# Conversion steps moved by one slot, and the first head pair's q and k turned in another order

## The chip, the cores and the metric

The kernel runs on one core of a Trainium2 chip. The metric is the device time in microseconds (us) of one execution. Below, PE is TensorE (matrix products), DVE is VectorE, ACT is ScalarE, POOL is GpSimd, and SP is SyncE, which only issues DMAs here.

## The reference

Attention with a threshold in place of a plain softmax, and then a two-layer MLP with an exact GELU on all tokens:

```python
batch, n_heads, seq, head_dim = (8, 8, 576, 64)
scores = np.matmul(q, k.transpose(0, 1, 3, 2)) / np.sqrt(64)
thresh = np.max(scores, axis=-1, keepdims=True) - tau
scores = np.where(scores >= thresh, scores, -1e9)
attn = np.exp(scores - max)                 # max: of each row
attn = attn / (np.sum(attn, axis=-1, keepdims=True) + 1e-09)
attn_out = np.matmul(attn, v)
x = attn_out.transpose(0, 2, 1, 3).reshape(8 * 576, 512)
h = x @ w_in                                # 512 x 2048
out = (0.5 * h * (1.0 + erf(h / sqrt(2)))) @ w_out   # 2048 x 512
```

The inputs q, k, v and tau are float32; the weights `moe_w_in` and `moe_w_out` are float64, and the kernel gets them as 64-bit words.

## The kernel before, in words

**Pairs and slots.** Two heads are worked on together: a head pair has 2 x 64 = 128 partitions, and there are 32 pairs, four for each batch. A row block of 128 queries is a chunk; the 576 queries of a head make four chunks and a tail of 64, and the tails of both heads share one chunk (chunk 4). A slot is one chunk of one pair. The program is written out slot by slot in a loop over `n`. The first four pairs (batch 0, "early") are done in two passes: slots 0 to 7 take chunks 0 and 1 of pairs 0 to 3, slots 8 to 19 chunks 2, 3 and 4 of pairs 0 to 3. From slot 20 on, each pair has five slots of its own.

**Work of a slot.** `scores` (line L432) multiplies the chunk's q with all k into PSUM, one bank pair for each head; there are two such buffers, so the scores of a slot wait until the slot before has read its own. `softmax_head` then takes the negative row maximum on DVE (L444, `nmx`), the threshold on POOL (L447, `thr`) and the exponential on ACT (L449). `softmax_tail` masks and sums on DVE (L465), which is the last reader of the scores. The result `p` is turned by PE products (L373) and copied by ACT (L380 to L395) into `pT`, and `weigh_v` multiplies it with v (L603, or L635 for half a block). Between these, `fill` puts in products of the MLP's first layer (L703, `hT`) and second layer (L718, `o_ps`), as many as a plan of due work (`GOAL`) allows. The first layer's results of the first block are kept until slot 20, where ACT loads another function table and does eight GELUs (L676), which the first L718 need.

**Turning q and k of the early pairs.** q and k arrive with tokens in partitions and must have the head dimension there. `turn_qk_early` does it with products by the identity (L324) into a PSUM bank `tr`, 8 calls (16 products in the profile) for each of q and k. The result is copied out: q by ACT with a scale (L327, `qT`), k by DVE for pair zero and by ACT else (L329, `kT`). The 64 tail rows are turned into another bank (L336 for zeros, L341), and ACT copies them out: twice for k (L344, L345), once for q (L348, `q_tail`). For pair zero, k comes first, then the tails, then q in two halves with a copy each; for the other pairs, q, k and the tails come in this order. The scale `q_scale` is worked out on DVE from `tau` (L1118 to L1122), which arrives by a DMA that POOL issues. Eight memsets on DVE (L1129) clear the q tails and the last column of v.

**Conversion of the weights.** A weight of 64 bits is turned into float32 on the chip, in 32 pieces of 128 x 512 numbers: 16 of w_in, 16 of w_out. One conversion step is L200 and L201 on ACT (`convert_first`), L208 and L209 on DVE (`convert_second`), and an addition L220 on POOL (`add_low_bits`). ACT's part runs one piece ahead. After DVE's part the next piece is loaded (`load_piece`, L184, issued by SP); eight loads are issued before the first conversion. POOL's additions belong to the next slot: the newest one right after its first row maximum and ahead of its threshold, the rest after the exponentials. How many steps stand at the end of slot `n` is written in a list:

```python
STEPS = [0, 1, 1, 1, 1, 1, 1, 1, 1, 2, 2, 2, 3, 2, 2, 3, 3, 3, 1, 0, 1]
```

In slots 12, 15 and 18, `convert_ahead(STEPS[n] - 1)` puts ACT's part earlier in the slot when more than one step is due.

**Order.** Nothing is scheduled by a tool: each engine runs its instructions in the order of the program, and waits by semaphores. In slots 18 and 19, DVE also turns k and q of pair 4 (L410; L415 and L420), which the scores of slot 20 need.

After slot 159 the last ten blocks of 256 tokens go through the MLP by nested Strassen-like products (L891), with sums on DVE and POOL (L773). The change doesn't reach that part.

Of the kernel before, what the change touches and what calls it, by code (L numbers as in the profile page):

```python
# [8 lines left out]
FP32 = mybir.dt.float32  # L9
U32 = mybir.dt.uint32  # L10
U8 = mybir.dt.uint8
AF = mybir.ActivationFunctionType
# [6 lines left out]
def kernel(  # L19
# [40 lines left out]
    TAIL = S - MAIN  # L60
# [19 lines left out]
    ps = ctx.enter_context(tc.tile_pool(name="ps", bufs=4, space=PSUM))  # L80
# [33 lines left out]
    def x_rows(i):  # L114
        return xall[:, i, :, :].rearrange("p c t -> p (c t)")
# [5 lines left out]
    ident = const.tile([P, P], FP32, name="ident")  # L121
# [3 lines left out]
    q_tail = [att.tile([P, P], FP32, name=f"q_tail{i}") for i in range(4)]  # L125
    v_sb = [att.tile([P, 2, KR, D], FP32, name=f"v{i}") for i in range(4)]
# [11 lines left out]
    q_scale = const.tile([P, 1], FP32, name="q_scale")  # L138
# [126 lines left out]
    def load_early(p):  # L265
        b, hp = divmod(p, HP)
        s = st[p] = {}
        for name, src in (("q", q), ("k", k)):

            if p == 2:  # L270
                at = s[name + "_slot"] = x_slot()
                t = x_rows(at)[:, 0:2 * (NC + 1) * D].rearrange("p (e c d) -> p e c d", e=2, d=D)
            else:
                t = ld.tile([P, 2, NC + 1, D], FP32, tag=name, name=name)
            s[name] = t
            eng = (nc.scalar, nc.gpsimd)[p] if p < 2 and name == "k" else nc.sync
# [23 lines left out]
    def turn_qk_early(p, names="qk"):  # L300


        s = st[p]
        if names == "k":
            qT, kT = s["qT"], s["kT"]
        elif 2 <= p < HP:
            qT = op.tile([P, MAIN], FP32, tag="o_sb", name="qT")
            kT = pd_tail[p - 2].rearrange("p b i -> p (b i)")
        else:
            qT = ld.tile([P, MAIN], FP32, tag="qT", name="qT")  # L310
            kT = ld.tile([P, TAIL + S], FP32, tag="kT", name="kT")
        s["qT"], s["kT"] = qT, kT
        qt = s["q_tail"] = q_tail[p % 4]
        copy = nc.scalar.copy if p else nc.vector.tensor_copy
        tiles = {name: s.pop(name) for name in names}

        def most(name, parts=1):
            t = tiles[name]
            tr = ps.tile([P, NC, P], FP32, tag="mm", name="tr")
            n = NC // parts  # L320
            for part in range(parts):
                for c in range(part * n, (part + 1) * n):
                    for e in range(2):
                        nc.tensor.matmul(tr[e * D:(e + 1) * D, c, :], lhsT=t[:, e, c, :], rhs=ident, start=True, stop=True)  # L324
                src = tr[:, part * n:(part + 1) * n, :].rearrange("p c s -> p (c s)")
                if name == "q":
                    nc.scalar.activation(qT[:, part * n * P:(part + 1) * n * P], src, AF.Copy, bias=0.0, scale=q_scale)  # L327
                else:
                    copy(kT[:, TAIL:S], src)  # L329

        def tails():
            tr = ps.tile([P, NC, P], FP32, tag="mm", name="tr")
            if "q" in names:
                none = q_tail[HP - 1][0:TAIL, D:2 * D]
                for e in range(2):
                    nc.tensor.matmul(tr[e * D:(e + 1) * D, 0, (1 - e) * TAIL:(2 - e) * TAIL], lhsT=ident[0:TAIL, 0:D],  # L336
                                     rhs=none, start=True, stop=True)
            for j, name in enumerate(names):
                for e in range(2):
                    at = e * TAIL if name == "q" else 0  # L340
                    nc.tensor.matmul(tr[e * D:(e + 1) * D, j, at:at + TAIL], lhsT=tiles[name][0:TAIL, e, NC, :],  # L341
                                     rhs=ident[0:TAIL, 0:TAIL], start=True, stop=True)
            if "k" in names:
                nc.scalar.copy(kT[:, S:S + TAIL], tr[:, j, 0:TAIL])  # L344
                nc.scalar.copy(kT[D:P, 0:TAIL], tr[D:P, j, 0:TAIL])  # L345
            if "q" in names:
                yield
                nc.scalar.activation(qt, tr[:, 0, :], AF.Copy, bias=0.0, scale=q_scale)  # L348
# [12 lines left out]
        x_free.extend(s.pop(name + "_slot") for name in names if name + "_slot" in s)  # L361

    def turn_p_early(p, i, later=None):

# [760 lines left out]
    load_early(2)  # L1125
    for _ in range(4):
        load_piece(nc.sync)
    for t in q_tail + [t[:, :, NC, :] for t in v_sb]:
        nc.vector.memset(t, 0.0)  # L1129
    turn_qk_early(0)  # L1130
    load_v_early(0)
    load_early(3)
# [2 lines left out]
    parts = [(range(2), HP), (range(2, SLOTS), HP)] + [(range(SLOTS), 1)] * (NP - HP)  # L1135
# [33 lines left out]
    for n in range(len(slots) + WEIGH + 1):  # L1169
        p, i = slots[n] if n < len(slots) else divmod(n, SLOTS)  # L1170
# [33 lines left out]
        if long:  # L1204
            convert_ahead(STEPS[n] - 1)
        if n in DIVIDE_LATE:
# [120 lines left out]
```

## Time and profile before

| | |
|---|---|
| runs shown, us | 1331.37, 1327.67, 1330.39; median 1330.39 |
| profiled execution, us | 1327.03 |
| its span, first to last instruction, us | 1325.3 |
| granted clock of PE | 1.000 |

The profile is of one execution, with times from the start of its span. Busy time is the time in which an engine executes an instruction; PE's busy time is modelled, since its products are pipelined. In a line of the timeline the columns are the start, the time from the first instruction's start to the last one's end, the engine, the line of the kernel's file, the operation, what it writes and reads, the shape, the number of instructions, and in brackets the idle time of the engine just ahead with what ended it, where there was any. The window 0 to 8.71 us, until the first scores, has PE busy for 6.83 us; from 98.76 to 105.57 us, between the scores of slots 17 and 18, it is busy for 5.00 of 6.81 us.

### The profile page before, as it was taken

The page shows a single profiled execution, that of the slowest core. Times are in us where ns is not written, and L with a number is a line of the kernel's source. Part 1 is how long each engine was busy: PE and PEld are TensorE (multiplying, and loading weights), DVE is VectorE, ACT ScalarE, POOL GpSimd, SP SyncE. Part 2 cuts the span into 40 slices and gives each one's busy share as a digit, 9 for nine tenths or more (in the row PEclk, how much of TensorE's full clock was granted, in tenths as well). Part 3 has the DMA queues.
Part 4 walks back from the last instruction along what each step waited for, and adds up shares of the span by engine and source line. Part 5 has one row for each costly group of instructions (what it writes and reads, how often), then busy time and mean ns, then how long its engine had stood idle before and what let it go on. Part 6 is the DMA issues. An engine that isn't in the chain of part 4 may idle for free.

```text
span 1325.3 us, 19980 instructions
## 1 busy us (share of the span) xinstructions
PE 1313.4 (99%) x6362; PEld 890.3 (67%) x6362; DVE 1042.8 (79%) x2009; ACT 601.9 (45%) x1018; POOL 634.2 (48%) x1058
## 2 busy tenths in 40 slices
PE   9999999999999999999999999999999999999998
PEld 7775476576476466466466466478778787877877
DVE  6888877888888888888888888883857698386674
ACT  7888266376376367357457438232111203211120
POOL 3565555465555555565555541236364403645430
PEclk9999999999999999999999999999999999999999
DMA  8453676767777777787787775400000140000003
GB/s 256 161 178 106 145 164 159 166 156 168 189 164 164 191 181 165 193 190 168 184 192 170 176 165 115 100 9 0 1 1 0 40 110 11 0 1 0 1 0 80
DMA packets 213688, 153.14 MB, mean 116 GB/s; under 512 B 117264, under 2 KB 196992, under 8 KB 213584
## 3 DMA queue, kind: packets, MB, share of 16 engines
q1 hardware_dynamic: 195440, 125.31, 40.4%
q0 software_dynamic: 17712, 26.26, 7.5%
q8 instruction: 52, 0.85, 0.3%
q14 instruction: 52, 0.43, 0.1%
q10 hardware_dynamic: 432, 0.30, 0.1%
HBM read 56.62 MB, written 12.58 MB: 52 GB/s over the span
## 4 chain that ended last, share of the span: by engine, by line
PE 93%; DVE 2%; issue 1%; DMA 1%; ACT 1%; POOL 1%; SPq 0%; POOLq 0%; DVEq 0%; ACTq 0%
PE bank L891 34%; PE o_ps L718 17%; PE hT L703 16%; PE sc L432 13%; PE xT L603 11%; PE tr L373 1%; DVE nmx L444 1%; PE xT L635 1%; PE tr L324 1%; DVE power L209 1%; DVE power L208 0%; ACT p L449 0%; DVE p L465 0%; DMA inv<-turned 0%; DMA turned_p<-in_moe_w_out_dram 0%
## 5 line engine op out<-in xcount | busy, mean ns | idle before, releaser
L449 ACT ACTIVATE p<-sc,nmx 128x576 f32<-128x576 f32 x288 | 201.9, 737 | 280.0 <-DVE nmx L444 279.8
L465 DVE SCALAR_TENSOR_TENSOR p<-sc,thr,p 128x576 f32<-128x576 f32 x288 | 225.2, 815 | 70.6 <-ACT p L449 62.2
L447 POOL TENSOR_SCALAR thr<-nmx,tau_eff 128x1 f32<-128x1 f32 x288 | 83.9, 293 | 333.3 <-DVE nmx L444 331.2
L703 PE MATMUL hT<-xall,w_in 128*128 128x256 f32 x1024 | 241.8, 385 | 0.0
L444 DVE TENSOR_REDUCE nmx<-sc 128x1 f32<-128x576 f32 x288 | 205.4, 750 | 41.9 <-PE sc L432 40.7
L718 PE MATMUL o_ps<-w_out,g 128*128 128x512 f32 x512 | 236.8, 603 | 0.0
L703 PEld LDWEIGHTS hT<-xall,w_in 128*128 128x128 f32 x1024 | 189.4, 190 | 51.3 <-issue 24.0
L773 DVE TENSOR_TENSOR o<-o,bank 128x256 f32<-128x256 f32 (+1 forms) x242 | 100.1, 417 | 94.5 <-PE bank L891 89.5
L773 DVE TENSOR_TENSOR c<-c,bank 128x320 f32<-128x320 f32 x304 | 147.2, 487 | 33.7 <-PE bank L891 20.1
L718 PEld LDWEIGHTS o_ps<-w_out,g 128*128 128x128 f32 x512 | 93.1, 190 | 109.5 <-issue 107.2
L432 PE MATMUL sc<-kT,qT 64*128 64x288 f32 x960 | 160.1, 429 | 1.5 <-DVE p L465 1.4
L564 DVE STREAM_TRANSPOSE turned_p<-p 128x1152 f32<-128x1152 f32 x112 | 154.4, 1378 | 3.9
L603 PE MATMUL xT<-pT,v 128*64 128x320 f32 (+1 forms) x1200 | 153.6, 410 | 0.0
L432 PEld LDWEIGHTS sc<-kT,qT 64*128 64x128 f32 x960 | 91.2, 186 | 75.9 <-issue 61.1
L603 PEld LDWEIGHTS xT<-pT,v 128*64 128x64 f32 x1200 | 83.4, 137 | 68.0 <-issue 10.4
L891 PE MATMUL bank<-w_out,c 128*128 128x256 f32 (+1 forms) x484 | 120.5, 379 | 0.8 <-DVE o L773 0.8
L261 POOL DMA_DIRECT2D v<-in_v_dram x208 | 110.8, 536 | 3.6 <-issue 1.4
L891 PEld LDWEIGHTS bank<-w_out,c 128*128 128x128 f32 x484 | 90.3, 190 | 19.0 <-DVE o L773 3.2
L958 ACT ACTIVATE c<-c 128x320 f32<-128x320 f32 (+1 forms) x80 | 46.8, 623 | 114.7 <-DVE c L773 114.7
L773 POOL TENSOR_TENSOR c<-c,g 128x320 f32<-128x320 f32 (+1 forms) x40 | 50.5, 1271 | 67.5 <-DVE c L773 67.5
L891 PE MATMUL bank<-t_out,g 128*128 128x256 f32 (+1 forms) x324 | 82.4, 377 | 0.4 <-DVE o L773 0.4
L891 PE MATMUL bank<-t_out,c 128*128 128x256 f32 x320 | 82.7, 381 | 0.0
(188 smaller groups left out, 1755.9 us busy)
## 6 DMA issues: line engine op xcount, KB each, us to landing
pT<-turned_p SPq DMA_DIRECT2D x448, 160.0 KB, 3.5
pT<-pd_tail SPq DMA_DIRECT2D x112, 80.0 KB, 3.0
q<-in_q_dram POOLq DMA_DIRECT2D x104, 72.0 KB, 3.7
k<-in_k_dram POOLq DMA_DIRECT2D x104, 72.0 KB, 3.2
inv<-turned SPq DMA_DIRECT2D x54, 128.0 KB, 4.1
v<-in_v_dram POOLq DMA_DIRECT2D x156, 40.0 KB, 3.1
out_dram<-o SPq DMA_DIRECT2D x40, 128.0 KB, 2.4
xall<-in_moe_w_out_dram SPq DMA_DIRECT2D x9, 512.0 KB, 4.8
```

Source lines behind the costliest of these rows:

```text
L261: eng.dma_start(t[r:P:4, e, 0:n, :], rows[:, r * KR:r * KR + n, :])
L432: nc.tensor.matmul(sc[e][:, h, 0:HALF], lhsT=lhsT, rhs=s["kT"][rows, at:at + HALF], start=True, stop=True)
L444: nc.vector.tensor_reduce(nmx[:, e:e + 1], sc, axis=AXIS.XY, op=ALU.max, negate=True)
L447: nc.gpsimd.tensor_scalar(thr[:, e:e + 1], nmx[:, e:e + 1], -1.0, tau_eff, op0=ALU.mult, op1=ALU.subtract)
L449: nc.scalar.activation(w[:, e * S:(e + 1) * S].rearrange("p (h s) -> p h s", h=2), sc, AF.Exp, bias=nmx[:, e:e + 1], scale=1.0)
L465: nc.vector.scalar_tensor_tensor(row, sc[e][:, :, 0:HALF], thr[:, e:e + 1], row, op0=ALU.is_ge, op1=ALU.mult, accum_out=den[e])
L564: nc.vector.transpose(turned_p[:, :, i // 2, 0:NB, i % 2 * Q:(i % 2 + 1) * Q], w.rearrange("p (e b i) -> p e b i", e=2, i=Q))
L603: nc.tensor.matmul(to, lhsT=s["v"][:, e, c, :], rhs=rhs, start=(c == 0), stop=(c == KR - 1))
L703: nc.tensor.matmul(hT[:, j % 2, :], lhsT=w_in_sb[c][:, j * P:(j + 1) * P], rhs=x_blk[n][:, c, :], start=(c == 0), stop=(c == N_DM - 1))
L718: nc.tensor.matmul(o[:, 0:d_model], lhsT=g[j][:, m * P:(m + 1) * P], rhs=w_out_sb[j], start=(j == 0), stop=(j == N_DF - 1))
L773: eng.tensor_tensor(out, a, b, op=ALU.add)
L891: nc.tensor.matmul(to, lhsT=l, rhs=r, start=start and k == 0, stop=k == len(pairs) - 1, skip_group_check=not start)
```

## The change

Three edits. In the list of conversion steps, slots 16 and 17 have two steps instead of three, slot 18 two instead of one, and slot 19 one instead of none. Pair zero is turned like the other pairs: q first with one copy, then k, then the tails; k's copy stays on DVE. The eight memsets on DVE move ahead of the four instructions that work out `q_scale` and `tau_eff`.

```diff
         copy = nc.scalar.copy if p else nc.vector.tensor_copy
-        tiles = {name: s.pop(name) for name in names}
-
-        def most(name, parts=1):
-            t = tiles[name]
+        for name in names:
+            t = s[name]
             tr = ps.tile([P, NC, P], FP32, tag="mm", name="tr")
...
-        if p == 0:
-            most("k")
-            rest = tails()
-            next(rest)
-            most("q", 2)
-            next(rest, None)
-            return
-        for name in names:
-            most(name)
-        for _ in tails():
-            pass
...
     load_early(0)
+    for t in q_tail + [t[:, :, NC, :] for t in v_sb]:
+        nc.vector.memset(t, 0.0)
     some = const.tile([P, 1], FP32, name="some")
...
-    for t in q_tail + [t[:, :, NC, :] for t in v_sb]:
-        nc.vector.memset(t, 0.0)
     turn_qk_early(0)
...
-    STEPS = [0, 1, 1, 1, 1, 1, 1, 1, 1, 2, 2, 2, 3, 2, 2, 3, 3, 3, 1, 0, 1]
+    STEPS = [0, 1, 1, 1, 1, 1, 1, 1, 1, 2, 2, 2, 3, 2, 2, 3, 2, 2, 2, 1, 1]
```

The products, copies and additions are otherwise the same, and so are the DMAs and their order. The line numbers in this document are those of the kernel before, unless it says otherwise.

More of the change, by code (lines that the diff above doesn't have):

```diff
@@ L314, in turn_qk_early @@
         copy = nc.scalar.copy if p else nc.vector.tensor_copy
-        tiles = {name: s.pop(name) for name in names}
-        def most(name, parts=1):
-            t = tiles[name]
+        for name in names:
+            t = s[name]
             tr = ps.tile([P, NC, P], FP32, tag="mm", name="tr")
[L320 to L334, printed above, removed]
-                for e in range(2):
[L336 to L348, printed above, removed]
@@ L350, in turn_qk_early @@
-        if p == 0:
-            most("k")
-            rest = tails()
-            next(rest)
-            most("q", 2)
-            next(rest, None)
-            return
-        for name in names:
-            most(name)
-        for _ in tails():
-            pass
-        x_free.extend(s.pop(name + "_slot") for name in names if name + "_slot" in s)
+            for c in range(NC):
+                for e in range(2):
+                    nc.tensor.matmul(tr[e * D:(e + 1) * D, c, :], lhsT=t[:, e, c, :], rhs=ident, start=True, stop=True)
@@ new lines, in turn_qk_early @@
+            src = tr.rearrange("p c s -> p (c s)")
+            if name == "q":
+                nc.scalar.activation(qT, src, AF.Copy, bias=0.0, scale=q_scale)
+            else:
+                copy(kT[:, TAIL:S], src)
+        tr = ps.tile([P, NC, P], FP32, tag="mm", name="tr")
+        if "q" in names:
+            none = q_tail[HP - 1][0:TAIL, D:2 * D]
+            for e in range(2):
+                nc.tensor.matmul(tr[e * D:(e + 1) * D, 0, (1 - e) * TAIL:(2 - e) * TAIL], lhsT=ident[0:TAIL, 0:D],
+                                 rhs=none, start=True, stop=True)
@@ new lines, in turn_qk_early @@
+        for j, name in enumerate(names):
+            t = s.pop(name)
+            for e in range(2):
+                at = e * TAIL if name == "q" else 0
+                nc.tensor.matmul(tr[e * D:(e + 1) * D, j, at:at + TAIL], lhsT=t[0:TAIL, e, NC, :],
+                                 rhs=ident[0:TAIL, 0:TAIL], start=True, stop=True)
+        x_free.extend(s.pop(name + "_slot") for name in names if name + "_slot" in s)
+        if "k" in names:
+            nc.scalar.copy(kT[:, S:S + TAIL], tr[:, j, 0:TAIL])
+            nc.scalar.copy(kT[D:P, 0:TAIL], tr[D:P, j, 0:TAIL])
@@ L363, in turn_p_early @@
+        if "q" in names:
+            nc.scalar.activation(qt, tr[:, 0, :], AF.Copy, bias=0.0, scale=q_scale)
     def turn_p_early(p, i, later=None):
```

## The prediction

> **What bounds the kernel now.** I read the engine shares first, then the timeline of the two places that the change touches, then the releasers of the idle time there.
>
> ```profile
> PE 1313.4 (99%) x6362; PEld 890.3 (67%) x6362; DVE 1042.8 (79%) x2009; ACT 601.9 (45%) x1018; POOL 634.2 (48%) x1058
> ```
>
> TensorE (PE) is busy 1313.4 of 1325.3 us. The change neither adds nor removes a matmul, so it can only give or take PE idle time, and there are about 12 us of that in all. The chain of waits is PE for 93%. The start, in the timeline of all engines:
>
> ```profile
> 4.17 1.98 PE L324 MATMUL tr<-ident,k 128*64 128x128 f32 x16
> ...
> 6.09 0.29 PEld L336 LDWEIGHTS tr<-q_tail,ident 64*64 64x64 f32 x4 [0.35 <-DVE q_tail L1129]
> ...
> 6.52 0.63 DVE L329 COPY kT<-tr 128x512 f32<-128x512 f32 x1
> ...
> 8.12 0.66 PE L324 MATMUL tr<-ident,q 128*64 128x128 f32 x8 [0.57 <-ACT qT L327]
> ...
> 8.71 1.24 PE L432 MATMUL sc<-kT,qT 64*128 64x288 f32 x8
> ```
>
> Columns are start and length. The tail products waited for a memset, the kT copy stood behind the other memsets, and the second half of q waited until ScalarE (ACT) had read the first half. The first scores start at 8.71. Then slots 16 to 21, engine by engine (PE, DVE, POOL, ACT):
>
> ```profile
> 103.05 0.71 PE L373 MATMUL tr<-ident,p 128*128 128x128 f32 x5
> 105.57 1.94 PE L432 MATMUL sc<-pd_tail,qT 64*128 64x288 f32 x8 [1.81 <-DVE p L465]
> ...
> 117.52 2.02 PE L373 MATMUL tr<-ident,p 128*128 128x128 f32 x14
> 119.47 1.24 PE L432 MATMUL sc<-kT,qT 64*128 64x288 f32 x8
> ```
> ```profile
> 101.71 0.42 DVE L208 TENSOR_SCALAR power<-power 128x512 uint32<-128x512 uint32 x1
> 102.17 0.69 DVE L209 SCALAR_TENSOR_TENSOR power<-xall,power 128x512 uint32<-128x512 uint32 x1
> ...
> 106.07 1.74 DVE L208 TENSOR_SCALAR power<-power 128x512 uint32<-128x512 uint32 x1
> ...
> 117.83 0.82 DVE L465 SCALAR_TENSOR_TENSOR p<-sc,thr,p 128x576 f32<-128x576 f32 x1 [1.07 <-POOL thr L447]
> ...
> 120.75 1.42 DVE L444 TENSOR_REDUCE nmx<-sc 128x1 f32<-128x576 f32 x2 [1.09 <-PE sc L432]
> ```
> ```profile
> 104.78 2.50 POOL L220 TENSOR_TENSOR w_out<-power,w_out 128x512 uint32<-128x512 uint32 x2
> ```
> ```profile
> 121.54 1.40 ACT L449 ACTIVATE p<-sc,nmx 128x576 f32<-128x576 f32 x2 [0.97 <-DVE nmx L444]
> ```
>
> Slot 18's scores (105.57) wait 1.81 us for slot 17's masking (L465), which frees the score banks. VectorE (DVE) is late because of conversions: it runs without a pause from 97.95 on. This is the longest PE wait of the execution after the start. From 119.47 PE stays fed, with two gaps of 0.2 us near 682 and 733 and three of 0.38 at the end.
>
> **What the Trainium skill says.** "TensorE: Matmul & The Clock Gate", section "Wait — 56ns, not 53.3ns?": a product of 128 columns takes 106.7 ns while the array is cold, 55.6 ns warm. The trace agrees: 16 took 1.98 us at 4.17, but 1.09 us at 9.88. Its Part 1 adds that the warm-up window runs freely, so the switch moves from run to run; here it lies between 6.1 and 6.9 us. "GPSIMD Engine Reference", "1. Specifications": GpSimd (POOL) shares SBUF access with DVE instructions in a two-port mode. The trace agrees: L208 takes 0.42 us alone and 1.74 at 106.07, when POOL's two adds last until 107.28. So a conversion's cost on DVE depends on POOL's backlog.
>
> **The change, part by part.** The sum is against the profiled execution: 1327.03 us, a span of 1325.3 and 1.7 around it. The median of the runs shown, 1330.39, is 3.4 above it.
>
> *Memsets first.* Eight memsets (1.15 us at 5.45) move to 1.25, into DVE's 3.57 us wait for tau. They end at about 2.4; tau lands at 4.80, and L1118 starts at 4.83 as before. Cost nothing, gain the 0.35 us wait and an unblocked kT copy. The trace doesn't show DVE memsets beside POOL's work at 1.27 to 4.3 (tau's and pair one's DMA issues, `ident`). If they held POOL for their whole 1.15 us, tau would land at 5.95 and pair one's last k at 9.1 instead of 7.98. The first is needed by qT's copy at 6.2, which itself has 1.2 us of slack, the second at 11.4 or later. I take 0.
>
> *q first, one copy.* PE: 16 q products at 4.17, cold, 1.65 to their last issue (q landed at 3.57 and 4.40). Then k from 5.83: some 7 cold and 9 warm, 1.25 us, to 7.1. Tails (their q landed at 6.40) 0.6, complete at 7.7. DVE's kT copy runs 7.4 to 8.03, beside the tails; ACT's one qT copy (0.68, from 6.2) lies beside the k products. ACT's two k tails, 0.21 each, run 7.8 to 8.2. First scores about 8.2 instead of 8.71: **gain 0.5 us**. If the array stays cold through k, 0.4 of it goes, so 0; at best 0.65. The chain from there (8.71 scores, L444, L449, L465, next scores) is shift-free, and the DMAs that later steps read have mostly landed before: pair one's by 8.19, pair two's by 9.97, v by 18.43 for 20.0.
>
> *STEPS.* A conversion is L200 and L201 on ACT (1.14 us from pair to pair, 1.29 to the pair's end), L208 and L209 on DVE (1.11 at best), L220 on POOL (1.27). No DMA moves: conversions through slot 15 number 24 in both kernels and 8 pieces are loaded ahead, so all 32 loads have been issued by then; SP's queue is unchanged. After slots 16 to 19 the totals are 27, 30, 31, 31 before, and 26, 28, 30, 31 after; slot 20 does the last in both. I follow the waits with the rows' own lengths (start, before and after):
>
> | event | before | after | set by |
> |---|---|---|---|
> | slot 17 L444 on DVE | 102.77 | 101.71 | third conversion gone |
> | slot 17 L465 | 104.59 | 103.53 | DVE's order |
> | slot 18 scores | 105.57 | 104.51 | L465 |
> | slot 18 L444 | 110.58 | 107.9 | two conversions, one POOL add less in the way |
> | slot 18 L465 | 112.38 | 109.6 | POOL's thr |
> | slot 19 scores | 113.96 | 112.9 | PE's own work |
> | slot 19 L465 | 117.83 | 116.05 | thr behind the add; ACT's exp |
> | slot 20 scores | 119.47 | 118.15 | PE's own work, its 0.3 wait for L465 gone |
> | slot 20 L444 | 120.75 | 119.4 | scores |
> | slot 20 L449 on ACT | 121.54 | 120.97 | ACT: moved L200, L201 |
> | slot 20 L465 | 122.58 | 121.75 | L449 |
> | slot 21 scores | 123.51 | 122.68 | L465 |
>
> So PE gains 1.06 at slot 18 and 0.3 at slot 20, and **gives about 0.5 back** at slot 21. There ACT's last pT copies end at 119.65 (120.57 before, 0.92 less), and the moved L200 and L201 stand between them and the exponential until 120.95, while the maximum that it waits for is there at 120.15. Before, ACT had 0.97 us of idle time here, which hides only part of it. Queued behind are the two exponentials, the GELUs (whose first result the products L718 need) and slot 21's scores. On DVE the moved conversion is covered by its 1.09 wait for scores; on POOL the add ends at 120.4, before the exponential. **Net gain 0.83 us**; the bounds are 1.35 (nothing given back) and the loss of the rival below. From slot 21 PE is fed and the lead reaches the end.
>
> Sum: 0.5 + 0.8 = 1.3 us, 1325.7 against 1327.03, or 1330.39 - 1.3 = **1329.1** as a median.
>
> **The rivals.**
>
> *Nothing reaches the end* (1330.4): the start's gain is eaten by a later switch of the array's clock, and the 1.81 wait is replaced by an equal one at slots 20 and 21. For it: ACT is busy 104.27 of the first 125.39 us, so its order matters as much as DVE's. Against: the 1.81 wait has a named cause, of which 1.1 leaves.
>
> *Slower* (1331.5), at slots 18 to 20. Slot 18 now converts two and slot 19 one. POOL's newest add (1.27 us) must follow the second conversion of slot 18 and stands ahead of slot 19's thr. If DVE doesn't run ahead in slots 16 and 17 (held by ACT or PE, not by conversions), slot 19's L465 comes one conversion later than 117.83, at 118.9, and the q transposes and slot 20's scores with it: +1.1. It decides from the point where slot 18's L465 comes later than 111.3 (112.38 less one conversion). I have 109.6, so 1.7 us of margin.
>
> *More* (1328.3): no give-back at slot 21 and the best start, 1.35 + 0.65 = 2.0.
>
> That the change doesn't do what it says is excluded by the built order: the moved instructions are these, PE's order differs only in pair zero, SP's nowhere.
>
> **How the numbers follow.** Main case 0.55, nothing 0.22, slower 0.15, more 0.08. All lie within 0.3% (4 us, about what a measurement of this kernel can tell from no change), and PE has little idle time to win. What lies outside comes from the scatter of the runs, 1327.67 to 1331.37, and from waits not foreseen: 0.06 faster, 0.11 slower, 0.83 same. The range is the runs' spread with the bounds on both sides: 1327.67 - 2.0 = 1325.7 to 1331.37 + 1.1 = 1332.5.
>
> **What would show it.** Right: first scores near 8.2; no PE wait over 1 us near 104; L208 after slot 17's masking under 1 us; the exponential of slot 20 straight after L201; L718 first near 124.6 less the start's half microsecond. Wrong: L718 first at 125.4 or later, or a PE gap at slot 20 or 21 of over 1 us.

## The result, and the profile after

The changed kernel takes **1325.77 us** (median of 9 runs, 1324.25 to 1326.43), the kernel before 1328.58 (9 runs on the same chip, 1326.6 to 1331.37). The ratio is 0.998, 95% interval 0.9971 to 0.9989: a small gain, below the 0.3% that the prediction took as about the least that a measurement of this kernel can tell; the interval lies clear of 1. The profiled executions are closer together than the medians: 1327.03 us before (span 1325.3), 1325.77 after (span 1324.0), so 1.26 us against 2.81 us. That difference is what the experiments had to settle. Line numbers past the turn of q and k are 18 lower after the change (L432, the scores, is L414; L465, the masking, L447; L449, the exponential, L431; L718, the second product, L700).

The engine shares of the page of the kernel after:

```profile
PE 1312.9 (99%) x6362; PEld 891.0 (67%) x6362; DVE 1041.1 (79%) x2009; ACT 602.4 (45%) x1017; POOL 635.7 (48%) x1058
```

The matmuls are the same in number, ScalarE (ACT) has one instruction less (one q copy for two), and of the 1.3 us by which the span is shorter TensorE's (PE) busy time makes 0.5 (1313.4 to 1312.9) and its idle time 0.8 (11.9 to 11.1). The start, in the timeline of all engines of the kernel after (start, length, engine, line, operation, idle time before and its releaser):

```profile
1.23 0.59 DVE L1100 MEMSET q_tail<- 128x128 f32 x4
...
4.17 1.45 PE L320 MATMUL tr<-ident,q 128*64 128x128 f32 x15
...
4.99 0.15 DVE L1102 TENSOR_SCALAR some<-tau_sb 128x1 f32<-128x1 f32 x1 [2.61 <-DMA tau_sb<-in_tau_dram]
...
5.48 1.12 PE L320 MATMUL tr<-ident,k 128*64 128x128 f32 x15
...
6.64 0.69 DVE L325 COPY kT<-tr 128x512 f32<-128x512 f32 x1 [1.00 <-PE tr L320]
...
7.48 1.39 PE L414 MATMUL sc<-kT,qT 64*128 64x288 f32 x8 [0.38 <-DVE kT L325]
```

The memsets lie in VectorE's (DVE) wait for tau, and tau's first reader starts at 4.99 (4.83 before), which nothing feels. The first scores start at 7.48 instead of 8.71. The k products take 1.12 us for 15, the warm rate; 16 took 1.98 before. So most of this lead is not less waiting: until the first scores PE is busy 5.79 of 7.48 us, and was 6.83 of 8.71 before, with 51 products in both. 1.04 of the 1.23 us are products that ran shorter, because the clock turned warm sooner in this execution. The last stretch of the change, slots 17 to 21, PE first, then DVE and ACT:

```profile
103.62 1.95 PE L414 MATMUL sc<-pd_tail,qT 64*128 64x288 f32 x8 [0.55 <-DVE p L447]
...
117.22 1.24 PE L414 MATMUL sc<-kT,qT 64*128 64x288 f32 x8
118.39 2.91 PE L585 MATMUL xT<-pT,v 128*64 128x320 f32 x20
121.72 1.94 PE L414 MATMUL sc<-kT,qT 64*128 64x288 f32 x8 [0.41 <-DVE p L447]
123.59 0.70 PE L700 MATMUL o_ps<-w_out,g 128*128 128x512 f32 x1
```
```profile
104.13 0.51 DVE L208 TENSOR_SCALAR power<-power 128x512 uint32<-128x512 uint32 x1
...
120.75 0.82 DVE L447 SCALAR_TENSOR_TENSOR p<-sc,thr,p 128x576 f32<-128x576 f32 x1 [0.46 <-ACT p L431]
```
```profile
118.60 0.69 ACT L200 ACTIVATE power<-xall 128x512 f32<-128x512 f32 x1
119.19 0.68 ACT L201 ACTIVATE w_out<-xall 128x512 uint32<-128x512 uint32 x1
119.90 1.37 ACT L431 ACTIVATE p<-sc,nmx 128x576 f32<-128x576 f32 x2
```

The wait of slot 18's scores fell from 1.81 to 0.55 us, L208 behind slot 17's masking from 1.74 to 0.51, and a new wait of 0.41 stands at slot 21, behind the exponential that starts when L201 ends. The lead of PE over the execution before, read at the same instruction in both:

| instruction | before | after | lead |
|---|---|---|---|
| first scores | 8.71 | 7.48 | 1.23 |
| idle products near 41 | 41.79 | 41.10 | 0.69 |
| slot 18's scores | 105.57 | 103.62 | 1.95 |
| slot 21's scores | 123.51 | 121.72 | 1.79 |
| a scores product near 147 | 147.09 | 145.33 | 1.76 |
| scores near 682, after their wait | 682.32 | 681.08 | 1.24 |
| scores near 733 | 733.00 | 731.76 | 1.24 |

Two pieces of lead are lost on the way: 0.54 between 8.71 and 41, and 0.52 between 147 and 682, of which a longer wait near 682 makes 0.27. The first is the wait for pair zero's v, in PE's timeline of the kernel before and of the kernel after:

```profile
20.02 1.31 PE L635 MATMUL xT<-pT,v 128*64 128x128 f32 x20
```
```profile
19.11 1.61 PE L617 MATMUL xT<-pT,v 128*64 128x128 f32 x20 [0.29 <-DMA v<-in_v_dram]
```

The products waited 0.29 us for the first of v's four parts, and took 0.30 longer while the others landed.

### The profile page after: what moved, and what is told of

It reads as the page before. It is cut to its first block, busy times and chain, and to the rows that moved or that the text cites. A ratio compares the mean times of both kernels' runs of the same rounds, so it can differ in the third digit from the quotient of the medians.

```text
span 1324.0 us, 19984 instructions
## 1 busy us (share of the span) xinstructions
PE 1312.9 (99%) x6362; PEld 891.0 (67%) x6362; DVE 1041.1 (79%) x2009; ACT 602.4 (45%) x1017; POOL 635.7 (48%) x1058
## 4 chain that ended last, share of the span: by engine, by line
PE 95%; DVE 1%; DMA 1%; ACT 1%; SPq 1%; issue 1%; POOL 0%; DVEq 0%; POOLq 0%; ACTq 0%
PE bank L873 34%; PE o_ps L700 17%; PE hT L685 16%; PE sc L414 14%; PE xT L585 11%; PE tr L355 1%; DMA v<-in_v_dram 1%; PE xT L617 1%; DMA xall<-in_moe_w_out_dram 0%; ACT p L431 0%; DVE nmx L426 0%; DVE power L209 0%; DVE p L447 0%; SPq L280 0%; DVE power L208 0%
## 5 line engine op out<-in xcount | busy, mean ns | idle before, releaser
L431 ACT ACTIVATE p<-sc,nmx 128x576 f32<-128x576 f32 x288 | 202.0, 738 | 278.0 <-DVE nmx L426 277.7
L447 DVE SCALAR_TENSOR_TENSOR p<-sc,thr,p 128x576 f32<-128x576 f32 x288 | 225.3, 816 | 71.4 <-ACT p L431 62.8
L700 PE MATMUL o_ps<-w_out,g 128*128 128x512 f32 x512 | 236.8, 603 | 0.0
L700 PEld LDWEIGHTS o_ps<-w_out,g 128*128 128x128 f32 x512 | 93.1, 190 | 109.5 <-issue 106.3
L414 PE MATMUL sc<-kT,qT 64*128 64x288 f32 x960 | 160.3, 429 | 2.4 <-DVE p L447 1.8
L414 PEld LDWEIGHTS sc<-kT,qT 64*128 64x128 f32 x960 | 91.7, 186 | 76.4 <-issue 61.8
```

The source lines that it names most:

```text
L414: nc.tensor.matmul(sc[e][:, h, 0:HALF], lhsT=lhsT, rhs=s["kT"][rows, at:at + HALF], start=True, stop=True)
L431: nc.scalar.activation(w[:, e * S:(e + 1) * S].rearrange("p (h s) -> p h s", h=2), sc, AF.Exp, bias=nmx[:, e:e + 1], scale=1.0)
L447: nc.vector.scalar_tensor_tensor(row, sc[e][:, :, 0:HALF], thr[:, e:e + 1], row, op0=ALU.is_ge, op1=ALU.mult, accum_out=den[e])
L700: nc.tensor.matmul(o[:, 0:d_model], lhsT=g[j][:, m * P:(m + 1) * P], rhs=w_out_sb[j], start=(j == 0), stop=(j == N_DF - 1))
```

## The experiments

Twelve runs follow, in three sets, each beside the kernel before, whose medians in the sets were 1328.2, 1328.26 and 1327.84. Each left one trace. Beside the median I give how many executions had a mean granted clock of TensorE of 0.998 or less. A cold stretch of 3.4 us at half clock takes 1.7 of 1324 us away, 0.0013 of the mean; the two traces that show such a stretch are the only two of the fourteen with a mean of 0.998 (all fourteen end at half clock, but after PE's last product). The mean doesn't see the start: until the first record of the clock the profile counts it as full (1.00 from 0 to 8.71 us in the kernel before, while 16 products take 1.98 us there).

### The start alone, and the steps alone

```diff
 # start_alone: the changed kernel
-    STEPS = [..., 2, 2, 2, 1, 1]
+    STEPS = [..., 3, 3, 1, 0, 1]
 # steps_alone: the kernel before
-    STEPS = [..., 3, 3, 1, 0, 1]
+    STEPS = [..., 2, 2, 2, 1, 1]
```

> The changed kernel's start (memsets first, q turned first with one copy) with the old list of conversion steps. Theory: the two parts of the change add. First scores near 7.5 us (8.71 before, 7.48 with the whole change); 0.7 us of lead is left from the wait for v at 19 us on; slot 18's scores wait about 1.8 us as before; the median is 0.5 to 0.7 us under the kernel before. Rival A: the start makes the whole measured 2.8 us between the medians, because the clock of the array in the kernel before turns warm later in most executions than in the profiled one; then this kernel takes 2 us or more. Rival B: the start's lead is used up at slot 18, where VectorE is late by its conversions; then the lead at slot 21 is 0 and the median the one of before.

> The kernel before with only the list of conversion steps changed (2, 2, 2, 1, 1 in slots 16 to 20). Theory: first scores near 8.7 us as before; the wait of slot 18's scores falls from 1.81 to about 0.55 us, slot 20's L373 wait of 0.14 goes, a wait of about 0.4 comes at slot 21; the lead there is 1.1 us and the median 0.8 to 1.1 under before. Rival A: the steps make most of the 2.8 us, since the 1.81 wait is longer in most executions than in the profiled one; then the median is 2 us or more under before. Rival B: without the start's lead the conversions of slots 16 and 17 are as late as before, and slot 18 gains less than 0.5.

Start alone: 1328.04 us (13 runs), ratio 0.9999, interval 0.999 to 1.0008. Steps alone: 1327.24 (13 runs), ratio 0.9995, interval 0.9986 to 1.0004. Neither can be told from no change, and their sum falls short of the 2.8 us. The start alone had first scores at 8.66 in its profiled execution, not at 7.5: its q products ran cold for 2.12 us where the changed kernel's took 1.45, with the same program up to there. From the timeline of the start alone:

```profile
4.17 2.12 PE L320 MATMUL tr<-ident,q 128*64 128x128 f32 x15
...
6.14 1.64 PE L320 MATMUL tr<-ident,k 128*64 128x128 f32 x15
```

What decided the case is slot 18 of this trace. PE's timeline, and then the table by windows (from:to, length, then busy us and count of PE, PEld, DVE, ACT and POOL, granted clock, share of DMA, GB/s):

```profile
105.19 2.75 PE L414 MATMUL sc<-pd_tail,qT 64*128 64x288 f32 x8 [1.54 <-DVE p L447]
107.88 3.74 PE L585 MATMUL xT<-pT,v 128*64 128x320 f32 x20
```
```profile
104.00:106.00 2.00, 0.79 (x4) 0.39 (x4) 1.96 (x6) 1.96 (x6) 2.00 (x4) 1.00 0.34 125
106.00:108.00 2.00, 2.00 (x8) 1.02 (x10) 1.97 (x2) 1.98 (x5) 1.15 (x2) 0.55 0.13 30
108.00:110.00 2.00, 2.00 (x10) 0.96 (x12) 1.93 (x5) 2.00 (x4) 0.00 (x0) 0.60 0.16 33
110.00:112.00 2.00, 2.00 (x16) 0.98 (x11) 1.62 (x3) 1.26 (x3) 1.57 (x3) 1.00 0.70 119
```

After the wait of 1.54 us the granted clock falls to half for 3.41 us (106.18 to 109.60), and the 20 products of p and v take 3.74 us instead of 2.91. The trace leads the kernel before by 0.38 us at slot 18's scores, and lags by 1.27 when these products are done: the stretch cost 1.65 us. In the profiled execution of the kernel before, the same wait, 1.81 there, was followed by a clock of 1.00. So the wait has a second price, which only some executions pay. 8 of the 13 runs of the start alone have the low mean clock (median 1329.14, the other five 1326.85), 3 of the 13 with the steps alone (1329.39, the other ten 1326.93). Of 158 executions of the kernel before in the three sets of runs, 86 have it (median 1329.36, the other 72 1327.17, so 2.2 us between them, of which one stretch explains 1.65); of the changed kernel's nine, none.

### The wait filled with work

```diff
 # before_filled: the kernel before; start_filled: start_alone
-    BUSY = {1: 2, 6: 2, 8: 2}
+    BUSY = {1: 2, 6: 2, 8: 2, 17: 12}
```

> The kernel before with 24 idle products of 128 columns (some 1.35 us) put on TensorE between slot 17's work and slot 18's scores, where it waits 1.81 us; nothing else is changed. Theory C: a wait of 1.5 to 2 us there turns the array's clock cold for about 3.4 us in some executions, as in the start alone's trace (granted clock 0.55 at 106 to 108 us), and costs them 1.3 us; the changed kernel takes that away beside the 1.3 us of its shorter waits. Then these products cost nothing (the scores still wait for the masking at 105.5) and the median falls from 1328.2 to about 1327.2, with hardly a run of a mean clock of 0.998 or less (26 of 50 in the kernel before). Rival: the low clock and the scatter come from the start or from later; then median and clocks stay as before, 1328.2. Second rival: the products end after the masking, and the kernel is 0.3 to 0.8 us slower.

> The start alone (old list of steps) with the same 24 idle products ahead of slot 18's scores. Theory C: the start's lead of about 0.7 us was hidden in the start alone's median (1328.04) by cold stretches after slot 18's wait; with the array kept warm the median is 0.5 to 0.8 under the one of the kernel before with the same products, so 1326.4 to 1326.8. Rival: the start's lead is eaten at slot 18 by VectorE's conversions or by a late switch of the clock at the start; then it equals the kernel before with these products, within 0.3.

Measured: 1332.14 us (8 runs), ratio 1.003 (1.0016 to 1.0043), and 1331.17 (22 runs), 1.0019 (1.0013 to 1.0026). The price was mis-sized: each product of this type is two records of 117 ns, 234 ns where I had counted 56, and they waited for a bank that ACT was still reading. PE in the kernel before with the products:

```profile
105.55 5.62 PE L298 MATMUL idle<-ident 128*128 128x128 f32 x48 [1.74 <-ACT g L670]
111.10 1.24 PE L432 MATMUL sc<-pd_tail,qT 64*128 64x288 f32 x8
```

5.62 us of work stood in the way, and slot 18's scores came 5.5 us later. They can't measure what the kept clock is worth. They do test the place: with 24 products right behind the wait (1.74 and 1.49 us), none of 30 executions has the low mean clock, against 86 of 158 and 8 of 13 without them. The start (old in one, new in the other) and everything behind slot 21 is as it was, so most of the low clocks of the kernel before come from slot 18. These kernels keep the wait and lack the cold stretch, so the wait alone doesn't make the array cold; the sparse work behind it takes part.

### The step that moved ahead of slot 20's exponential

```diff
 # step_in_20 and steps_23201: the changed kernel
-    STEPS = [..., 2, 2, 2, 1, 1]
+    STEPS = [..., 2, 2, 2, 0, 2]      # step_in_20
+    STEPS = [..., 2, 3, 2, 0, 1]      # steps_23201
```

> The changed kernel with slot 19's conversion moved to slot 20 (2, 2, 2, 0, 2): L200 and L201 then stand behind slot 20's exponential on ScalarE instead of ahead of it. Theory: the 0.41 us wait of slot 21's scores is made by these two; the exponential starts near 119.3 instead of 119.90, slot 21's scores near 121.3 without a wait, and the median falls by 0.4. Rival A: the wait stays, since the masking of slot 20 waits for the threshold from GpSimd or for VectorE; nothing changes. Rival B: two conversions in slot 20 bring two adds on GpSimd ahead of slot 21's threshold, and a wait of 0.5 to 1.5 us comes at slot 22; slower than the changed kernel by up to 1.

> The changed kernel with the steps 2, 3, 2, 0, 1 in slots 16 to 20 instead of 2, 2, 2, 1, 1: one conversion goes from slot 19 to slot 17, and ScalarE's L200 and L201 no longer stand ahead of slot 20's exponential. Theory: the 0.41 us wait of slot 21's scores is made by these two instructions and goes (slot 20's exponential near 119.3); but slot 18's masking gets VectorE's 1.1 us of conversion back, so slot 18's scores wait 1.5 us or more instead of 0.55, and the net is 0.5 to 0.8 slower than the changed kernel in its profiled execution and more in the median, through cold stretches. Rival: the conversion in slot 17 hides behind TensorE's work, slot 18's wait stays near 0.6, and the kernel is 0.4 faster.

step_in_20: 1330.13 us (14 runs), ratio 1.0015 (1.0006 to 1.0024), 4.4 us above the changed kernel. Its first half confirms the give-back: without L200 and L201 ahead of it the exponential starts at 118.80 and slot 21's scores follow without a wait. Its second half is the price, in ACT's and PE's timelines:

```profile
118.80 1.41 ACT L431 ACTIVATE p<-sc,nmx 128x576 f32<-128x576 f32 x2 [0.71 <-DVE nmx L426]
...
121.52 4.27 ACT L658 ACTIVATE g<-g 128x512 f32<-128x512 f32 x8
...
127.21 0.65 ACT L200 ACTIVATE power<-xall 128x512 f32<-128x512 f32 x1
```
```profile
131.74 1.49 PE L414 MATMUL sc<-kT,qT 64*128 64x288 f32 x6 [1.96 <-DVE p L447]
```

The last L200 now stands behind the GELUs, until 127.21; DVE's L208 waits 3.61 us for it, the maximum of slot 21 stands behind that on DVE, and the next scores wait 1.96 us near 130. The place is that of rival B, the engine isn't: ACT, not GpSimd (POOL). Nor is the size: B had a wait of up to 1.5 us and a loss of up to 1 us. 11 of the 14 runs have the low mean clock: again a kernel with a long wait of PE.

steps_23201: 1325.72 us (22 runs), ratio 0.9981 (0.9974 to 0.9988), level with the changed kernel. Slot 18's wait stayed at 0.53, so my theory of it fell: the masking that this wait is for stands ahead of the conversions of slot 17. Slot 21's wait went as expected, but the third conversion of slot 17 came back as two other waits, 0.26 us at 112.59 (behind ACT) and 0.17 at 117.64 (behind DVE). From 41 to 146 us this order gains 0.78, the changed kernel's 1.07. Its trace holds the second cold stretch, far from slot 18. The table by windows:

```profile
680.00:682.00 2.00, 1.11 (x5) 0.33 (x3) 0.75 (x2) 0.00 (x0) 1.96 (x5) 1.00 0.84 243
...
684.00:686.00 2.00, 2.00 (x6) 1.63 (x5) 1.79 (x5) 1.87 (x3) 0.58 (x2) 0.50 0.87 258
```

A wait of 1.11 us at 681 is followed by the half clock from 683.83 to 687.25, and between 683.4 and 687.1 PE loses 1.69 us against the kernel before. What makes this wait is the last point below.

### The switch of the clock at the start

```diff
 # warm5: the changed kernel
-    for _ in range(3):
+    for _ in range(5):
         nc.tensor.matmul(idle, lhsT=zeros[:, 0:P], rhs=zeros, ...)
```

> The changed kernel with five instead of three warm-up products at the start (TensorE busy from 1.31 to about 4.1 us instead of 2.93). Theory: the switch to the warm clock needs a stretch in which the array is busy; with no idle time ahead of the q products it comes no later than 5.4 us in nearly all executions, first scores at 7.2 to 7.5; the median falls by 0.2 to 0.5, since the lead is capped by the wait for v at 19 us. Rival: the switch lies at a time of its own, whatever is issued at 3 to 4 us; first scores scatter between 7.4 and 8.7 as they do now and the median is unchanged.

1325.93 us (22 runs), ratio 0.998 (0.9972 to 0.9988): the changed kernel's time. The test was mis-sized. I had read 2.93, the length of the warm-up products in the timeline, as their end. They end at 4.24 in the changed kernel, so PE is not idle ahead of q there, and two more delay q. PE's timeline of this kernel:

```profile
1.31 4.42 PE L147 MATMUL idle<-w_out 128*128 128x256 f32 x10 [1.31 <-DVE w_out L144]
5.66 1.09 PE L320 MATMUL tr<-ident,q 128*64 128x128 f32 x16
6.58 1.04 PE L320 MATMUL tr<-ident,k 128*64 128x128 f32 x16
```

q and k are both warm here, but begin 1.49 us later, and the first scores come at 8.51. So the run itself says nothing on what sets the switch. What the other traces show is how far it moves. In the eight traces with the new turn of q and k and three warm-up products, the first scores lie at 7.40, 7.48 and 7.56 (15 q records took 1.37 to 1.54 us), at 8.36 to 8.70 in four (2.12 to 2.43 us, cold throughout), and at 8.35 in steps_23201, where q landed late (a wait of 0.73). Their mean is 8.11. The five with the old turn lie between 8.52 and 8.87, mean 8.69. The Trainium skill's "TensorE: Matmul & The Clock Gate", Part 1, says that the warm-up window runs freely; a switch that moves by a microsecond under one program agrees with it.

The traces also hold a record of every switch of the clock. Between the first and the last, the times between switches are whole multiples of 3.413 us in all fourteen: 29 of them from 7.20 to 106.18 in start_alone, 199 from 4.58 to 683.83 in steps_23201, and one for each cold stretch. What differs from execution to execution is where this grid lies. The first switch to the full clock, with three warm-up products, falls between 4.48 and 7.20 us, and with the new turn the first scores follow it (steps_23201, where q landed late, is left out):

| | switch | first scores |
|---|---|---|
| v_first, after, step_in_20 | 4.48, 4.77, 5.02 | 7.40, 7.48, 7.56 |
| start_filled, turn_steps, v_first_23201, start_alone | 6.47, 6.58, 6.94, 7.20 | 8.36, 8.39, 8.70, 8.66 |
| old turn: before_filled, steps_alone, memsets_steps, before, before_again | 4.49, 4.50, 6.27, 6.62, 6.66 | 8.75, 8.52, 8.59, 8.71, 8.87 |

With the old turn an early switch gains nothing: in steps_alone (4.50) the 16 k products took 1.25 us, and the time went into a wait of 0.79 us for the memset. So the new turn is worth some 1.2 us at the first scores when the switch comes early, and 0 to 0.3 when it comes late.

### Memsets or turn

```diff
 # memsets_steps: the kernel before with the new STEPS, and
+    for t in q_tail + [...]: nc.vector.memset(t, 0.0)   # moved here, behind load_early(0)
 # turn_steps: the changed kernel
+    for t in q_tail + [...]: nc.vector.memset(t, 0.0)   # moved back, ahead of turn_qk_early(0)
```

> The kernel before with the new steps and the memsets first, but with pair zero turned k first and q in two halves as before. Theory: the 0.35 to 0.8 us wait of the tail products for a memset goes, the 0.57 wait for ScalarE's first half of q stays, first scores at 8.1 to 8.6 with a switch of the clock near 6.5; the median lies between the steps alone (1327.24) and the changed kernel (1325.77), near 1326.5, and few of the runs show a mean clock of 0.998 or less. Rival: all of the start's gain comes from the memsets; then the median is 1325.8. Second rival: none of it does, and it is 1327.2.

> The changed kernel with its memsets back where they were (after the tau scalars, ahead of pair zero's turn), so q first with one copy and the new steps. Theory: with q first the tail products come at 6.5 or later, when the memsets (5.45 to 6.6) are nearly done, and VectorE's kT copy waits for TensorE until 6.6 anyway; so the memsets' place is worth at most 0.2 us and the median equals the changed kernel's, 1325.6 to 1326.1. Rival: the memsets delay the kT copy and the tail products whenever the clock turns warm early; then it is 0.5 to 1 us slower than the changed kernel, 1326.3 to 1326.8.

Memsets with the steps: 1327.21 us (21 runs), ratio 0.9995 (0.9988 to 1.0003), the time of the steps alone. In its trace the wait for the memset is gone, the 0.57 for ACT's first half of q is there, and first scores start at 8.59. Turn with the steps: 1325.67 us (11 runs), ratio 0.9988 (0.9976 to 1.0), the time of the changed kernel; first scores at 8.39. So the turn does what the start does, and the memsets' place shows nothing in the median, once q comes first. Three of the eleven runs of turn_steps have a low mean clock (1329.11, 1330.73, 1330.74); no trace shows one of them. With the old turn, at the high mean clock, memsets_steps has 1326.49 (16 runs) and the steps alone 1326.93 (10), so whether the memsets' place is worth something there stays open.

### v of pair zero earlier

```diff
 # v_first: the changed kernel; v_first_23201 has the steps 2, 3, 2, 0, 1 as well
     load_early(2)
+    load_v_early(0)
     for _ in range(4):
         load_piece(nc.sync)
     turn_qk_early(0)
-    load_v_early(0)
```

> The changed kernel with pair zero's v loaded ahead of the first four weight pieces on SyncE's queue (one line moved up). Theory: half of the start's lead of 1.26 us is lost at 19.1 us, where the products of p and v wait for v of pair zero; with v there in time the lead at 41 us is 1.2 to 1.3 instead of 0.69, and slot 21's scores come 0.3 to 0.5 earlier than 121.72. Median 0.3 to 0.5 under the changed kernel. Rival: the lead is lost to something else near 20 us (p's transposes, their copies); then L617 waits for that at the same time and nothing is gained. Second rival: the pieces land later by v's own transfer, the first conversions come late, and slots 1 to 3 lose what is gained.

> The changed kernel with pair zero's v loaded ahead of the first four weight pieces, and the steps 2, 3, 2, 0, 1. Theory: v in time keeps 0.6 us of the start's lead, the moved step takes the wait of slot 21's scores away (0.4); with the earlier lead the wait near 680 us for the landing of the reciprocals grows in part, so the median is 0.3 to 0.9 under the changed kernel, 1324.9 to 1325.5, and faster than both kernels. Rival: the DMA that GpSimd waits for near 676 us sets the time from there on in most executions; then the median stays at 1325.6 to 1325.9.

v_first: 1325.82 us (21 runs), ratio 0.9984 (0.9978 to 0.9991): nothing gained on the changed kernel. v had landed by 13.21 instead of 19.58, PE didn't wait for it, and the idle products started at 40.47, a lead of 1.32. But step_in_20, with v in its old place and first scores at 7.56, also kept 1.18 of lead there: its v landed between 17.87 and 18.65 and was first read at 18.84. In the changed kernel's execution the four parts were issued from 10.99 on and landed between 18.98 and 19.58, in that of the kernel before from 10.16 on, between 18.22 and 18.86. Even with the same issue the landing moves: the first part, issued at 10.22 in step_in_20 and at 10.23 in start_filled, landed at 17.87 and 18.84. So the loss of 0.54 belongs to one execution, not to the kernel.

v_first_23201: 1327.26 us (13 runs), ratio 0.9989 (0.998 to 0.9998), 1.4 us slower than either of its two halves. Its trace has first scores at 8.70 and a wait of 1.30 at 681; why nearly all its runs are slower (12 of 13 with the high mean clock, 1327.08) stays open. No version that was run beats the changed kernel.

### The kernel before, once more

> The kernel before, unchanged, as a run of its own. Theory: half or more of its executions show a mean clock of 0.998 or less, and lie near 1328.5 to 1331; those at 0.999 or 1.000 have a median of 1327.1 to 1327.4. If the profiled one is of the first kind, TensorE's granted clock is about 0.5 to 0.6 for some 3.4 us right after slot 18's wait near 105 us, or from the start to later than 7 us, and nowhere else for as long. Rival: the profiled one has a low mean clock with warm windows at 102 to 112 us; then slot 18 is not the cause of the scatter. The ratio is 1.000 within 0.001.

1327.65 us (13 runs), ratio 1.0004 (0.9994 to 1.0015). 5 of the 13 have the low mean clock (median 1330.34), the others have 1327.24. The profiled one isn't of the first kind: slot 18's scores waited 1.81 us as in the first profile, and the clock stayed at 1.00. So no trace shows a cold stretch of the unchanged kernel. That they lie behind slot 18 rests on the start alone's trace, on the filled wait, and on how the share of low mean clocks follows the wait of slot 18's scores:

| kernels | wait in the trace, us | low mean clock |
|---|---|---|
| the kernel before | 1.81 | 86 of 158 |
| start_alone | 1.54 | 8 of 13 |
| steps_alone, memsets_steps | 0.75, 0.76 | 8 of 34 |
| both parts: the changed kernel, warm5, steps_23201, turn_steps, v_first, v_first_23201 | 0.52 to 0.55 | 6 of 98 |
| before_filled, start_filled: 24 products behind it | 1.74, 1.49 | 0 of 30 |

(step_in_20, with 0.54 here, has its wait of 1.96 us further on.) Why one execution pays and the next doesn't is not shown, but the grid of 3.413 us gives a hint. In its step from 102.20 to 105.61, which holds the whole wait, the profiled kernel before had PE busy for 1.60 us and stayed warm; in the step ahead of the cold stretch of start_alone (102.77 to 106.18) PE was busy longer, 1.86 us. But apart from transposes, 0.71 us in both, 1.02 us of the first were products of the first layer, which use all 128 rows and columns, and 0.34 of the second. It is the same near 681: 2.30 us busy, 0.49 of it first layer, ahead of the cold stretch of steps_23201 (680.42 to 683.83), and 2.23 and 1.10 in a step of v_first that stayed warm (680.33 to 683.75). So how long PE idles doesn't decide it; what its products are may. No run tested this.

### The wait near 681

Over the fourteen traces this wait of PE has no fixed length: 0 in five, 0.18 to 0.48 in four, 1.11 to 1.70 in five. POOL's order in v_first (1.48 there) shows what it hangs on:

```profile
676.37 1.69 POOL L633 TENSOR_TENSOR xall<-xall,inv 128x128 f32<-128x128 f32 x3 [1.95 <-DMA inv<-turned]
...
678.01 2.15 POOL L261 DMA_DIRECT2D v<-in_v_dram  x4
680.20 0.31 POOL L429 TENSOR_SCALAR thr<-nmx,tau_eff 128x1 f32<-128x1 f32 x1
```

The multiplication by the reciprocals waits for their DMA, four issues of v's loads (2.15 us) follow, and only then comes the threshold for which DVE's masking and then PE's scores wait. In the kernel after, POOL was released 0.95 us after its last work, here after 1.95. In all fourteen traces PE's wait is what POOL idles ahead of and between these multiplications less 0.43 to 0.48 us (0.68 gave 0.21, 0.95 gave 0.48, 1.95 gave 1.48, 2.00 gave 1.54; under 0.35 there is none). The v loads and the threshold need nothing from that DMA; they only stand behind it. No run changed this order.

## Why the prediction was right, point by point

Forecast: 1329.1 us [1325.7, 1332.5]; measured 1325.77, inside the range by 0.07 us. That it is inside is luck: the gain of 2.81 is over twice the forecast, and the lower end was the lowest of three runs less the best case. The difference of 3.3 has three terms. The three runs first shown had a median of 1330.39, nine had 1328.58: **1.81**. The low-clock executions of the kernel before, which the change takes away: 1328.58 against 1327.17 without them, **1.41** (the nine runs have no clock on record; 1327.17 is that of the 72 executions with a high mean clock in the three later sets). The rest is 0.1: at a high mean clock the two kernels stand at 1327.17 and 1325.77, a difference of 1.40 where the sum was 1.3. Of the signs, those of the steps came: a wait of 0.55 us near 104, L208 in 0.51, the exponential straight after L201, L718 first at 123.59 (124.1 was named). That of the start didn't: the first scores came at 7.48, not near 8.2.

- **"It can only give or take PE idle time".** Wrong, and most of what was not foreseen comes from here. The number of products is the same, but not their time: at the start 1.04 of 1.23 us are shorter products, and a cold stretch lengthens products by 1.65 us.
- **Memsets, cost nothing.** Right: first tau reader at 4.99 for 4.83, no releaser moved. The gain that I gave them (0.35) is nothing once q is turned first.
- **Start, 0.5 us.** In the profiled pair it was 1.23; between the means of eight and five traces, 0.58. That the mean is near the forecast is luck. The case that it describes, a switch among the k products, is that of start_filled and turn_steps: first scores at 8.36 and 8.39, a gain of 0.3. "Cold through k" is nearly that of start_alone: 8.66, a gain of 0, as said. Missing is the early switch, ahead of all k products, with a gain of 1.2 where "at best 0.65" was allowed: I had read the switch (6.1 to 6.9 us) in one execution, and in the changed kernel's it came at 4.77.
- **"The chain from there is shift-free".** Wrong for the profiled execution by 0.54: v, "18.43 for 20.0", was late by 0.29 at 19.11, and its later parts by 0.30 more. 18.43 is the landing of the second of four parts, the last came at 18.86; and I compared the slack with a lead of 0.5 and one landing, where the lead was 1.23 and the landing moves by 1 us.
- **Steps, net 0.83.** Measured 1.07 (1.76 less 0.69), and 0.90 with the steps alone (1.08 less 0.18). The table of events holds: less the 0.69 of lead, slot 18's scores came 1.26 earlier (forecast 1.06), slot 20's 1.56 (1.32), the exponential 0.95 (0.57), slot 21's scores 1.10 (0.83). The give-back, forecast 0.5, was 0.46 (1.56 less 1.10), by the pair L200 and L201 as said; step_in_20 took them away and the wait went. The term that was too small is slot 18's, by 0.2, and not through the conversion: from slot 16's masking to slot 17's maximum DVE took 5.56 us before and 4.53 after, 1.03 less for a forecast of 1.06. With the steps alone slot 18's scores gained 1.07. The rest belongs to the turn. ACT's first copy of slot 16, before and after, stands behind products (L373) that begin at 93.14 and 92.45:

```profile
94.11 1.07 ACT L380 COPY pT<-tr 128x512 f32<-128x512 f32 x2 [0.77 <-PE tr L373]
```
```profile
93.14 1.07 ACT L362 COPY pT<-tr 128x512 f32<-128x512 f32 x2 [0.49 <-PE tr L355]
```

It starts 0.97 us after them in all five traces with the old turn, 0.69 in all nine with the new, and with it slot 16's exponential and masking and slot 18's scores move by 0.2 to 0.3: their wait is 1.81 without either part, 1.54 with the new turn, 0.75 with the new steps, 0.55 with both. So the two parts meet at slot 18, which the prediction kept apart. What holds ACT's copy is open.

- **"The lead reaches the end".** Wrong by 0.52. Of that 0.27 is the longer wait at 681, and 0.25 came off gradually between 133 and 680, which no run explains. I read the gaps near 682 and 733 in one execution as fixed; the first scatters from 0 to 1.70.
- **The rivals.** "Nothing reaches the end" fell, "slower" too: slot 18's masking came at 108.71 against the 111.3 from which it would decide. "More" (2.0) was nearest to the median, by a way that it didn't name. The missing rival was that a wait of PE costs more than its length. The Trainium skill's rule in "TensorE: Matmul & The Clock Gate", "HAM oscillation — how this bites in real kernels", is to have no idle gaps above about 3.4 us; here 1.54 and 1.11 us, each with sparse work around it, were followed by 3.4 us at half clock. The measurement decides: the rule's bound is not safe in this kernel.

What stays open: single parts at the high mean clock gained 0.3 (start, 5 runs) and 0.2 (steps, 10), together 1.4. The 0.27 at slot 18 is the one coupling that the traces show. For the rest: two kernels with both parts, whose traces stand 0.68 us apart at slot 21's scores, have medians of 1325.37 (turn_steps, 8 runs) and 1327.08 (v_first_23201, 12 runs) at the high mean clock, so a difference of 1 us between two kernels says little about the part in which they differ.

## What to carry to other kernels

Price a wait of the matmul engine twice: its length, and the chance that the clock falls behind it. Compare executions of one mean clock first, then count how many fall out of it; here half of the 2.8 us was found only by the count. When a lead is to be carried past a transfer, set it against the scatter of the landing over several traces, not against one landing; and before a conversion step is moved, follow it on each engine to the next instruction that somebody waits for, since the same step cost 0.4 us of waits in slot 17 or slot 19, and 4 us in slot 20, where its first half stood behind the GELUs on ScalarE.

## What was not expected of the hardware

- A wait of PE of 1.1 to 1.5 us can be followed by 3.41 us at half clock, which cost 1.65 us at slot 18 and 1.69 near 684. It doesn't always follow: eleven waits of over 1 us past the start in the fourteen traces, two cold stretches.
- The switch to the warm clock at the start moved by a microsecond and more under the same program: 15 q records took 1.37 us in one execution and 2.43 in another. All later switches are whole multiples of 3.413 us behind it.
- DMAs issued at the same place land far apart from execution to execution: v of pair zero by 1 us with the same time of issue, and the last of the four transfers of the reciprocals near 676 took 4.0 to 7.8 us from issue to landing.
